# One upright pair fewer in the second pass, new operation times and a new order table in a clustered attention and softplus FFN kernel

## The chip, the cores and the metric

The kernel runs on one core of a Trainium2 chip. The metric is the device time of one execution in microseconds (us). Before the change three runs gave 825.47 us as their median, from 823.66 to 826.16.

## The reference

Attention in which a query sees only the keys of its own cluster, and behind it a feed-forward layer (FFN) with softplus. With 4 batches, 8 heads, 768 positions, head size 64 and 16 clusters, cut to what is computed:

```python
q_n, k_n, c_n = (x / (norm(x) + 1e-6) for x in (q, k, centroids))
q_assign = argmax(einsum('bhsd,hcd->bhsc', q_n, c_n), -1)     # k_assign likewise
mask = q_assign[:, :, :, None] == k_assign[:, :, None, :]
scores = where(mask, q @ k.T / 8, -1e9)
attn = exp(scores - max(scores)); attn = attn / (sum(attn) + 1e-9)
x = (attn @ v).transpose(0, 2, 1, 3).reshape(3072, 512)
h = x @ w_in                                                  # 3072 x 2048
out = (max(h, 0) + log1p(exp(-abs(h)))) @ w_out               # 3072 x 512
```

Products of float32 operands are made from pairs of float16 halves: each operand is cast to a high half, and the rest is subtracted into a low half.

## The kernel before

**The work.** A *pass* is half the queries of one batch: 3 of its 6 blocks of 128 queries. There are 8 passes. Within a pass, each of the 8 heads gives 3 *tiles* (one block of 128 queries against all 768 keys), so there are 192 tiles, numbered `t` in the order pass, head, block. Tiles 0 to 23 are the first pass, 24 to 47 the second. A tile is named by head and block: `s_3_5` is tile 35. Behind the attention of a pass come its FFN1 (`ffn1`, L1205: 16 blocks of 24 matmuls of `h`), softplus (`softplus`, L1234) and FFN2 (`ffn2`, L1280: `o`), which run beside the attention of the next passes.

**Two forms of a tile.** `scores` (L1044) makes the scores of a tile and `attend` (L1125) weights the values with them.

- The *ordinary* form: four matmuls of scores (L1064, `s`), the row maximum on VectorE (L1080, `negm`), the exponential on ACT (L1086), a cast to the high half (`ph`, the cast of L298, on ACT unless moved) and a subtraction for the low half (`p`, L1100, on POOL unless moved). When both tiles of a pair (`t`, `t + 1`) are done, one DMA turns the pair's halves (L1110, `pt<-phl`), and 18 matmuls of float16 halves weight the values (L1148 to L1150).
- The *upright* form (`upright`, L947): two matmuls give the scores of the high halves alone (L957, `m`), VectorE takes their maximum (L969, `negu`), TensorE turns the 128 maxima from a column into a row (L976, into the PSUM tile `turned`), and ACT or VectorE copies that row, scaled, into a spare row of the turned queries (L982 or L984, `qt<-turned`; the operation `u`). Twelve matmuls then give scores that are already shifted and already turned (L996 and L997, `u`), the exponential goes straight to float32 probabilities, and six records of float32 matmuls weight the values (L1144). No cast, subtraction or DMA is needed.

`UPRIGHT` (L33) lists the pairs in upright form: 0 to 17, so tiles 0 to 35. The copy of L976's result must be done before the twelve matmuls. `turned` is one PSUM tile with four places, `turned[:, hk[2] % 4]` (L972).

**The masks.** `nearest` (L561) assigns keys and queries to their clusters with chains of VectorE operations (L593 to L613), for each pair of heads of keys and each four heads of queries; `keep` (L920) and `clusters` (L709) drop clusters without a key. A DMA (`fill`, L553) clears the spare row of queries whose tiles are ordinary but share a group of heads with upright ones.

**The weights** of the FFN come as float64 and are made float16 halves in steps (`prep_weights`, L377) in the first part of the run.

**The order.** All engines execute their instructions in the order in which the program emits them. Each piece of work is a generator that yields operations, waits and ring requests. The class `Order` (L110) runs them: the table `PLAN` (L44) gives, two base-36 digits at a time, the number of the channel whose next operation is emitted (3304 entries). So the table sets the order on every engine, on the SP queue (which issues the DMAs) as well. Operations carry a cost in ns with which `Order.run` keeps a model time per engine; it is used for one thing while emitting: where the model sees a gap on TensorE of over 400 ns, `warm` (L271) puts dummy matmuls (L277, *fillers*) there. A ring (`ring`, L305) makes a channel wait until an earlier user of the same place is done; it holds the emission back, not the chip.

`either` (L288) gives an operation two engines; its key in `SWAPPED` (L39) picks the second. A `cast` (L295) is such an operation: ACT first, POOL second.

Of the kernel before, what the change touches and what calls it, by code (L numbers as in the profile page):

```python
# [29 lines left out]
ROWS = EXTRA + 1  # L30
UP = 8
UPRIGHT = (0, 1, 2, 3, 4, 5, 6, 7, 8, 9, 10, 11, 12, 13, 14, 15, 16, 17)
# [6 lines left out]
SWAPPED = ('g0_3', 'g0_5', 'g1_1', 'g2_5', 'g6_6', 'g6_7', 'g7_1', 'g7_2', 'g7_4', 'g7_7', 'gh1_6', 'gh2_4', 'gh3_1', 'gh6_7', 'gh7_0', 'gh7_2', 'gh7_3', 'gh7_5', 'gh7_6', 'gh7_7', 'k0_0', 'k0_1', 'k14', 'k18', 'k22', 'kT0_0_0', 'kT0_2_1', 'kT1_2_0', 'kT1_2_1', 'm12_2_0', 'm12_3_0', 'm20_4_0', 'm8_2_0', 'm8_3_0', 'p100', 'p101', 'p103', 'p136', 'p38', 'p39', 'p40', 'p42', 'p45', 'p46', 'p47', 'p59', 'p61', 'p64', 'p67', 'p71', 'p72', 'p79', 'p82', 'p85', 'p89', 'p90', 'p92', 'ph58', 'ph62', 'ph83', 'ph86', 'ph87', 'q0_0_0', 'qT1_1', 'u1', 'u11', 'u13', 'u21', 'u23', 'u27', 'u31', 'u33', 'u35', 'v8', 'vh14', 'vh18', 'w15', 'w19', 'w20', 'w23', 'w29', 'wh17', 'wh24', 'wh29', 'wh30', 'wh7', 'wh9', 'x0_2', 'x2_0', 'xh0_3', 'xh1_3', 'xh2_3', 'xh3_0', 'xh3_3', 'zk10', 'zk12', 'zk16', 'zk18', 'zk2', 'zk20', 'zk4', 'zq0_1', 'zq8_2')  # L39
# [5 lines left out]
    "020306c30004050cd10a0000000000000000000101d300d4d20005c4060607070c050100d50001010101d1d1d106d2d2d1d2d6d2d1c5"  # L45
    "0101010101d8d706060c07d1d1d7d2d1d1d1d106d2d1d2d20a0606060606d2d1d2d20101c305d906dadad2d2c4c5d1d10106dcc4d107"
    "d10606c51f1fd2d21h1hd21fd2c608081f05080b0b0bc70adb0908c80b1h1j1j1h1f1f1j1l1l1h1h1jc4c3c3c51g1n1l1j1n1i080808"
    "1n090909c31j1l1p1l081n1p0ac61k070a1l09c30808c7080cc41r1r0b0b0b0b1n1p1pc908cacb0b1t1r1r0cdddd1m0b1t0909091n1p"
    "1pc51t1o1rc81t1rc90bdf090909091vdedhc4c5dfdhdhdh1v1q1q1q1qdidididjdidg1x1t1t1v1v1q1q1scc1qdkcd1x1z1z1x1vca1x"
    "1v1u1z1xc7c6c61zc61xc8c7c7c6c721211w23231z21211z1y210d252023ce0bcfc9cac8cbcc21caca25252723c822c9c9c8ca2723c9"  # L50
    "23252927270d2b2222222925cdce25242b2b29272d29260d0dcccbcccecd2d2729292fcf222b28ccce2f2h2f0d2d2f2d2bcb22cccgch"
    "ci2h2j2a0d0d0dcgcg2b2dcf0dcf0d0dcd2j2c2h2d2f2e0dcf0dcf0d0d22cjcd2fcbcb2h2e2e2e2l2j2j0d0d2l2n2nchci2echcgch2g"
    "2h2h2j2l2n2lcgcgck2jch2nce2p2p2i2l2k2p2l2r2ncicicjci2p2rcdchcl2ncjcj2m2p2t2r0eckckckck2t2p2rcj2e2ecicmcjce2o"
    "2r2r2v2v2t2q2t2v2t2q2q2qcl2x0e0e0e2v2tck2q2q2s2v2v2x2z2z2x2xcmclcmclcm2ucn2q2z312x312w0e0e0e0e0e0e0eco2z2x2z"
    "cl2z330e333131cl2y310fcncn0ecncz33353531cmcmcpcq33czcncococo33dncn35cz37370f0f0fcococrczdododn35303937320e0e"
    "0e0e333537dncz0hdododo3232323439czcp32cqcpcqcpcq32323537390f0f3b3936dqdqdqczcpcp3739crcq3b0fcrcrcrcr393d0fcz"
    "3bcz3b0ecs3d3d3b0f0f0f3dczdrdr0h3bdsds0f0fdrdr0hcqdr383d0i3d3f3f3aczctcscsdscs3f3h3f3f3c3jcz3edt3h3jcscs0gcu"
    "0i0i0i3h3ld03hductct3h3hdu3educz3j0g3n3e3e3educzd0ctcu3l3ndt0i3j3l3pdwdwct3e3edud0cu0g0j0kcucu3l3n3ndwczczdx"
    "3gdx0i3p0i0icz3rczctcucv3l3j3l3p3t3p0g3ndxczdx0i3r3iczdxd03p3pcvdydy3t3r3v0idycz3kdz0jcvcv3tcz3xcvdz3te03md0"
    "0j3vcvcw3t3rdz3x3r3t3v3z3zczdzdze1e1e1e10k0k0k3x3ocze2cw3q3qcz413q3qcwcw0i3ze2e2e2cxcze33qd00n3x0i0i3ve3cwcz"  # L60
    "cwe2d0cze5e53x3s3v3x3qe3e4d0410mcye5czczcxcxcxcxcxe40g3u0ke5e5e6d0e7e741410ke7cz0k0k0k0k0k413z3z410k0n0n3q0n"
    "d0cze9e9e90m0m0ld0e9e9e8d0ea3w0g0g0g0gcycy0gcycy0g0g0gcyd03yd040e80g0g0g0g0ld0420od0424242424242ebeb0n0n0n0n"
    "0n0n0n0n0l0l0n0kd0d04343434343ecd0cz454545454545ecczed4747474747cz494949494949edd0eeczefef4b4b4b0o0oedd04d4d"
    "4defefd00l0l0l0l4f4f0l0ld04b4b4d4d4f444h4h4h4hd0egeg4j4j4j464dcz0l0l0l0l4h4l4l4f4fefczeheheh48cz4a4hcz0l4n4n"
    "cz4l4p0pcz0l4ceieieicz4p4e4e4l4l4j4j4lej4neieiejej4e4e4p4p4pczd0cz4g0p0pek4e4e4eekekek4n4nekczelel4r4r4r4iee"
    "4p4t4t4tczd0elel4v4v4r4r4k4x4x4t4t4v4v4v4x4mczemem4t4z4zczemem51514zczenen4o0p534q4qen4x4x4xcz51d04q4q4q4q53"
# [116 lines left out]
def tile_cluster_attention__then__softplus_ffn(  # L183
# [1050 lines left out]
    def softplus(pi, f, hp, hk):  # L1234
# [31 lines left out]
        if not two:  # L1266
            yield cast(f"gh{pi}_{fp}", 830, 1290, gh[:, 0], g)
# [138 lines left out]
```

## Time and profile before

| what | value |
|---|---|
| median of 3 runs | 825.47 us |
| the profiled execution's own time | 827.26 us |
| its span in the trace | 825.4 us |
| TensorE matmul (PE) busy | 809.5 us, 7919 instructions |
| VectorE (DVE) busy | 522.1 us |
| ScalarE (ACT) busy | 537.0 us |
| GpSimd (POOL) busy | 458.7 us |
| granted TensorE clock | 1.0 in every stretch of 20 us |

How to read the rows that follow: in a group (`L1080 DVE ... x156 | 148.3, 953 | 57.3 <-PE`) stand line, engine, operation, output and inputs with shapes, the count, then the busy us, the mean ns of one, and the idle us just ahead of the group's instructions with what ended most of it. In a timeline a row is start (us), length (us), engine, line. In a table of stages a row is the stretch, its length, then busy us and count of PE, PEld (weight loads), DVE, ACT and POOL, then the granted clock, the share of the DMA engines and GB/s. Matmuls overlap, so their work is taken from start to next start, and not from the length.

### The profile page before, as it was taken

What the parts mean: (1) busy time and instruction counts of PE and PEld (TensorE: products, weight loads), DVE (VectorE), ACT (ScalarE), POOL (GpSimd) and SP (SyncE); (2) the same over time, 40 slices, a digit from 0 to 9 for tenths busy, and PEclk for the clock granted to TensorE, in tenths of its full rate; (3) what the DMA queues carried; (4) which work ended last, traced back from release to release, by engine and by line L of the source; (5) the groups of instructions that cost most, each with busy time, mean ns of one, the idle gap of its engine ahead of it and who ended that gap; (6) DMA issues with size and microseconds to landing.
All of it is one profiled execution on the core that took longest, in us unless ns stands there. A gap on an engine that the chain in (4) does not pass through costs nothing.

```text
span 825.4 us, 19143 instructions
## 1 busy us (share of the span) xinstructions
PE 809.5 (98%) x7919; PEld 525.8 (64%) x7919; DVE 522.1 (63%) x909; ACT 537.0 (65%) x830; POOL 458.7 (56%) x341
## 2 busy tenths in 40 slices
PE   7999999999999999999989999999999999999998
PEld 7888987655666666566656656556666656655554
DVE  6789998877876877666785557577555444332222
ACT  5776789865877777558578677767766668622220
POOL 4753556444756576655667685677576666611120
PEclk9999999999999999999999999999999999999999
DMA  8986768999999999998799999999889787530001
GB/s 236 239 197 138 204 158 218 213 212 197 179 177 174 179 207 201 212 197 170 153 166 172 183 171 208 199 197 172 171 158 163 136 138 134 118 54 14 26 1 39
DMA packets 389816, 133.69 MB, mean 162 GB/s; under 512 B 367072, under 2 KB 382688, under 8 KB 389728
## 3 DMA queue, kind: packets, MB, share of 16 engines
q1 hardware_dynamic: 389728, 132.46, 81.3%
q8 instruction: 62, 1.02, 0.5%
q14 instruction: 26, 0.21, 0.1%
HBM read 35.68 MB, written 6.29 MB: 51 GB/s over the span
## 4 chain that ended last, share of the span: by engine, by line
PE 86%; DVE 5%; DMA 4%; ACT 2%; issue 1%; POOL 0%; SPq 0%; DVEq 0%; ACTq 0%; POOLq 0%
PE s L1064 11%; PE h L1219 9%; PE h L1221 9%; PE h L1220 9%; PE o L1303 9%; PE o L1305 9%; PE o L1304 9%; PE mbank L1144 5%; PE mbank L1150 3%; PE mbank L1148 3%; PE mbank L1149 3%; DMA pt<-phl 2%; DMA kt<-kn 1%; PE u L996 1%; PE u L997 1%; PE m L957 1%
## 5 line engine op out<-in xcount | busy, mean ns | idle before, releaser
L1100 POOL TENSOR_TENSOR phl<-p,phl 128x768 f16<-128x768 f32 x133 | 220.3, 1664 | 145.5 <-ACT phl L298 98.8
L1080 DVE TENSOR_REDUCE negm<-s 128x1 f32<-128x768 f32 x156 | 148.3, 953 | 57.3 <-PE s L1064 57.0
L1086 ACT ACTIVATE p<-s,negm 128x768 f32<-128x768 f32 x156 | 139.5, 895 | 68.7 <-DVE negm L1080 56.4
L1221 PE MATMUL h<-xT,wi 128*128 128x384 f16 x512 | 166.8, 326 | 0.0
L1220 PE MATMUL h<-xT,wi 128*128 128x384 f16 x512 | 166.7, 326 | 0.0
L1219 PE MATMUL h<-xT,wi 128*128 128x384 f16 x512 | 166.7, 325 | 0.1
L1303 PE MATMUL o<-wo,gh 128*128 128x512 f16 x376 | 142.4, 379 | 0.4 <-DVE ot L1352 0.4
L1305 PE MATMUL o<-wo,gh 128*128 128x512 f16 x376 | 142.5, 379 | 0.0
L1304 PE MATMUL o<-wo,gh 128*128 128x512 f16 x376 | 142.4, 379 | 0.0
L298 ACT CAST phl<-p 128x768 f16<-128x768 f32 x151 | 123.8, 829 | 19.2 <-DMA pt<-phl 16.3
L1252 DVE SCALAR_TENSOR_TENSOR fg<-fa,h 128x384 f32<-128x384 f32 x128 | 70.1, 549 | 103.9 <-ACT fa L1241 95.9
L1240 ACT ACTIVATE fa<-h 128x384 f32<-128x384 f32 x128 | 62.3, 487 | 111.0 <-PE h L1221 110.6
L1064 PE MATMUL s<-kt,qt 128*128 128x384 f16 x624 | 127.0, 326 | 2.4 <-ACT p L1086 2.4
L1272 POOL TENSOR_TENSOR gh<-fg,gh 128x768 f16<-128x768 f32 x54 | 89.3, 1657 | 29.5 <-ACT gh L298 28.2
L1148 PE MATMUL mbank<-vb,pt 128*128 128x65 f16 x936 | 101.3, 192 | 0.5 <-DMA pt<-phl 0.5
L1149 PE MATMUL mbank<-vb,pt 128*128 128x64 f16 x936 | 101.4, 192 | 0.0
L1150 PE MATMUL mbank<-vb,pt 128*128 128x65 f16 x936 | 101.0, 194 | 0.0
L1148 PEld LDWEIGHTS <-pt 128*128 128x128 f16 x936 | 86.9, 98 | 14.2 <-DMA pt<-phl 2.6
L1149 PEld LDWEIGHTS <-pt 128*128 128x128 f16 x936 | 86.3, 97 | 11.4
L1150 PEld LDWEIGHTS <-pt 128*128 128x128 f16 x936 | 86.5, 97 | 0.0
L1064 PEld LDWEIGHTS <-qt 128*128 128x128 f16 x624 | 58.3, 98 | 43.2 <-issue 3.1
L1221 PEld LDWEIGHTS <-wi 128*128 128x128 f16 x512 | 49.9, 98 | 33.2
(180 smaller groups left out, 1307.3 us busy)
## 6 DMA issues: line engine op xcount, KB each, us to landing
wo<-in_moe_w_in_dram SPq DMA_DIRECT2D x16, 512.0 KB, 5.4
wo<-in_moe_w_out_dram SPq DMA_DIRECT2D x14, 512.0 KB, 4.3
out_dram<-ot SPq DMA_DIRECT2D x23, 256.0 KB, 2.6
rawk<-in_k_dram SPq DMA_DIRECT2D x15, 384.0 KB, 4.2
rawq<-in_q_dram SPq DMA_DIRECT2D x15, 384.0 KB, 4.4
rawv<-in_v_dram SPq DMA_DIRECT2D x12, 384.0 KB, 4.0
rawv<-in_v_dram SPq DMA_DIRECT2D x8, 192.0 KB, 6.1
pt<-phl SPq DMA_TRANSPOSE x78, 5.9
```

Source lines behind the costliest of these rows:

```text
L1064: nc.tensor.matmul(st[:, j, :SH], qt[:, s, i], kt[:, s, NT // 2 * j : NT // 2 * (j + 1)], start=(s == 0), stop=(s == 1),)
L1080: yield op("DVE", 950, lambda: nc.vector.tensor_reduce(negm, st[:, :, :SH], AX.XY, ALU.max, negate=True))
L1100: lambda e: e.tensor_tensor(phl[:, u, 1], p32, phl[:, u, 0], ALU.subtract),
L1148: nc.tensor.matmul(av, pt[:, 0, c], vb[:, c, D : 2 * D + 1], start=(c == 0), stop=False)
L1149: nc.tensor.matmul(av[:, :D], pt[:, 0, c], vb[:, c, :D], start=False, stop=False)
L1150: nc.tensor.matmul(av, pt[:, 1, c], vb[:, c, D : 2 * D + 1], start=False, stop=(c == NT - 1))
L1219: nc.tensor.matmul(hp, w[0], x[0], start=(c == 0), stop=False)
L1220: nc.tensor.matmul(hp, w[0], x[1], start=False, stop=False)
L1221: nc.tensor.matmul(hp, w[1], x[0], start=False, stop=(c == NP - 1))
L1303: nc.tensor.matmul(po, g[0], wo[:, f, 0, 0], start=(f == f0), stop=False)
L1304: nc.tensor.matmul(po, g[0], wo[:, f, 0, 1], start=False, stop=False)
L1305: nc.tensor.matmul(po, g[1], wo[:, f, 0, 0], start=False, stop=(f == f0 + NF // 2 - 1))
```

## The change

Pair 17 (tiles 34 and 35: head 3, blocks 4 and 5, in the second pass) is made in ordinary form. The costs of some operations are set to other numbers. The ring of turned maxima has size 1, so that a turning is emitted only after the copy of the one before is. `SWAPPED` (103 keys, now 143) and `PLAN` (3304 entries, as before) are replaced as a whole.

```diff
-UPRIGHT = (0, 1, 2, ..., 14, 15, 16, 17)
+UPRIGHT = (0, 1, 2, ..., 14, 15, 16)
...
-SWAPPED = ('g0_3', 'g0_5', 'g1_1', 'g2_5', 'g6_6', 'g6_7', ...
+SWAPPED = ('g0_1', 'g0_5', 'g0_7', 'g1_1', 'g1_7', 'g2_0', ...
...
-    "020306c30004050cd10a0000000000000000000101d300d4d20005c4060607070c050100d50001010101d1d1d106d2d2d1d2d6d2d1c5"
+    "020306c30405000a07d10101d3d4000000000000000000000006060101d5000100d1d1d2d201060101010cd2d1d1d1060101d101d1d1"
...
-        yield cast(f"wh{step}", 655, 890, part[:, 0], val)
+        yield cast(f"wh{step}", 655, 720, part[:, 0], val)
...
-            ("DVE", 640),
+            ("DVE", 690),
...
-        yield cast(f"vh{n}", 830, 1290, vb[:, :, :, D : 2 * D], vf)
+        yield cast(f"vh{n}", 830, 870, vb[:, :, :, D : 2 * D], vf)
...
-            ("DVE", 950),
+            ("DVE", 1000),
...
-        yield either(f"zk{n}", last[:2], ("ACT", 310), mark, **here)
+        yield either(f"zk{n}", last[:2], ("ACT", 370), mark, **here)
...
-        hk = yield from ring("mT", 4)
+        hk = yield from ring("mT", 1)
         ps = turned[:, hk[2] % 4]
...
-        yield either(f"u{t}", ("ACT", 250), ("DVE", 190), shift)
+        yield either(f"u{t}", ("ACT", 265), ("DVE", 290), shift)
...
-            yield cast(f"ph{t}", 830, 1290, parts[0], p32)
+            yield cast(f"ph{t}", 830, 870, parts[0], p32)
...
-        yield cast(f"xh{pi}_{pr}", 510, 690, by_head[0], x32)
+        yield cast(f"xh{pi}_{pr}", 510, 510, by_head[0], x32)
```

The other casts and subtractions get the same new numbers (1290 to 870, 950 to 1000, 540 to 560; 220 to 270 for the marks of the first queries). The last two numbers of a cast are its costs on ACT and on POOL.

What the new tables come to, counted in the two programs: L1064 has 632 matmuls where it had 624, L957 68 (72), L976 34 (36), L996 and L997 204 each (216), L1144 204 (216), L1148 to L1150 948 each (936), and the fillers of L277 are 175 (200). 34 more casts stand on POOL, and 32 fewer on ACT: 18 of `phl`, 4 of `gh`, 5 of `xn`, 2 of `wo`, 2 of `wi`, 2 of `kn` and 1 of `vb`. VectorE has 9 more subtractions of L1272 (19 where 10 stood) and 3 fewer of L1100 (20 where 23 stood). The SP queue has one more transposition of a pair and one more clearing of a spare row. All 34 turnings of maxima (L976) stand in the order of their tiles. The rows below show two places, as the programs emit them.

On VectorE, what stood before where tile 35 (head 3, block 5) has its maximum; `negu` is an upright tile's maximum, `mx_k8`, `eq_k8` and `best_k8` are key masks, `wo` is a weight step:

```order
L969 TENSOR_REDUCE negu_3_4_1996<-m_3_4_1944 128x1
L597 TENSOR_REDUCE mx_k8_1993<-sim_k8_1928 128x12
L414 TENSOR_SCALAR wo_120<-wo_120 128x512
L418 SCALAR_TENSOR_TENSOR wo_120<-wo_120 128x512
L603 TENSOR_TENSOR eq_k8_2036<-sim_k8_1928,mx_k8_1993 128x192
L969 TENSOR_REDUCE negu_3_5_2044<-m_3_5_2034 128x1
```

After, on the same engine at the same tile (`negm` is an ordinary tile's maximum, `p32` the probabilities in float32, `phl` the pair of their halves, `fg` of the softplus):

```order
L1080 TENSOR_REDUCE negm_3_5_2008<-s_3_5_2000 128x1
L1252 SCALAR_TENSOR_TENSOR fg_0_1_1970<-fa_0_3_1985,h_0_3_1972 128x384
L609 TENSOR_TENSOR eq_k8_2010<-eq_k8_2010,tab_78 128x192
L1100 TENSOR_TENSOR phl_3_4_2001<-p32_3_4_1998,phl_3_4_2001 128x768
L1100 TENSOR_TENSOR phl_3_4_2001<-p32_3_5_2037,phl_3_4_2001 128x768
L611 TENSOR_REDUCE best_k8_2067<-eq_k8_2010 128x12
```

The maximum of tile 35 became one of full scores, and the two low halves of tiles 34 and 35 (L1100) came in on VectorE behind it, ahead of the last operations of a key mask.

On TensorE, before, where tiles 15 and 16 (head 5, blocks 0 and 1) are turned:

```order
L1144 MATMUL mbank_117<-rawv_4_132,ptf_4_0_1165 128x65 x6
L976 MATMUL turned_116<-eye32_100,negu_5_1_1188 65x128
L976 MATMUL turned_116<-eye32_100,negu_5_0_1172 65x128
L996 LDWEIGHTS kt_4_593
L996 MATMUL u_4_2_1219<-qt_4_0_610,kt_4_593 128x128
```

After, at the turning of tile 16 on the same engine (`m` are the scores of an upright tile's maximum):

```order
L1144 MATMUL mbank_117<-rawv_4_132,ptf_4_0_1127 128x65 x6
L976 MATMUL turned_116<-eye32_100,negu_5_1_1160 65x128
L957 LDWEIGHTS qt_4_0_549
L957 MATMUL m_6_0_1199<-kt_6_543,qt_4_0_549 128x384
L957 LDWEIGHTS qt_4_0_549
```

Tile 15's turning, which stood right behind that of 16, now stands 31 rows ahead of it, and other work lies between the two.

More of the change, by code (lines that the diff above doesn't have):

```diff
@@ L50 @@
[L50 to L54, printed above, removed]
@@ new lines @@
+    "1r1v0909df09dh1vdic90c0c0cc51r1tcac71q1q1q1qdhdhdh1v1t1x1xdidic6di1vc81t1qc91q1s1v1z1x1zc71x1vc908dgcbdjdec7"
+    "c71u211z1x1z1x21c8c6c81wcc0b1z2121ca23231zc8cdc7ca1y25210dc6c6cecb25202321c9cacacac8cc2327222325272922222222"
+    "2229c9cd23252b2b270d0d2725dk1qcf0d2924cececc2dcd2dc9cecbcc25272927262b2b2fcfcbcf2f2929280d2d0d2bcccbcb0d0d0d"
+    "0d2a2h0d2hcfcdce2d2f2b2d2c2jcgcgcgch0d0dcfcecf2j0d2d2e2e2e2e2f2h2f2h2f0d0d0d2j2j2l2l2n2ncicjch2ecdci0d2g2l2l"
+    "2h2h2n2jcgcg2p2n2jchcicgck2pcjchcicjcccj2i2p2l2l2k2p2n2r2rchchclcici2ncd2e2m2t2p2r0e222tckckck2pcm2rcjckcj2o"
@@ L644, in prep_k @@
         else:
-            yield cast(f"kh{n}", 830, 1290, n1[:, :, :D], kf)
+            yield cast(f"kh{n}", 830, 870, n1[:, :, :D], kf)
             yield either(
@@ L648, in prep_k @@
                 ("POOL", 1640),
-                ("DVE", 950),
+                ("DVE", 1000),
                 lambda e: e.tensor_tensor(n1[:, :, D:], kf, n1[:, :, :D], ALU.subtract),
@@ L697, in low_half @@
             ("POOL", 910),
-            ("DVE", 540),
+            ("DVE", 560),
             lambda e: e.tensor_tensor(dst[:, :, D:], src, dst[:, :, :D], ALU.subtract),
@@ L767, in prep_q @@
         if pi == 0:
-            yield cast(f"qh{sfx}", 850, 1290, n1[:, :, D:], qf)
+            yield cast(f"qh{sfx}", 850, 870, n1[:, :, D:], qf)
             yield either(
@@ L771, in prep_q @@
                 ("POOL", 1640),
-                ("DVE", 950),
+                ("DVE", 1000),
                 lambda e: e.tensor_tensor(n1[:, :, :D], qf, n1[:, :, D:], ALU.subtract),
@@ L802, in prep_q @@
         )
-        yield either(f"zq{sfx}", last[:2], ("ACT", 310), mark_queries(n2[:, :, ROWS : ROWS + NCL], sim), **here)
+        yield either(f"zq{sfx}", last[:2], ("ACT", 370), mark_queries(n2[:, :, ROWS : ROWS + NCL], sim), **here)
         wide = ROWS if n < H else D
@@ L863, in first_q @@
             ("POOL", 910),
-            ("DVE", 540),
+            ("DVE", 560),
             lambda e: e.tensor_tensor(lo, x, hi, ALU.subtract),
@@ L878, in first_q @@
         )
-        yield either(f"zq0_0_{u}", last[:2], ("ACT", 220), mark_queries(n2[:, part, ROWS : ROWS + NCL], sim), **here)
+        yield either(f"zq0_0_{u}", last[:2], ("ACT", 270), mark_queries(n2[:, part, ROWS : ROWS + NCL], sim), **here)
         yield wait("al", 2 * u)
@@ L1031, in upright @@
                 ("POOL", 1640),
-                ("DVE", 950),
+                ("DVE", 1000),
                 lambda e: e.tensor_tensor(parts[1], p32, parts[0], ALU.subtract),
@@ L1094, in scores @@
         phl, phlk = pair[t // 2]
-        yield cast(f"ph{t}", 830, 1290, phl[:, u, 0], p32)
+        yield cast(f"ph{t}", 830, 870, phl[:, u, 0], p32)
         yield either(
@@ L1098, in scores @@
             ("POOL", 1640),
-            ("DVE", 950),
+            ("DVE", 1000),
             lambda e: e.tensor_tensor(phl[:, u, 1], p32, phl[:, u, 0], ALU.subtract),
@@ L1183, in attend @@
             ("POOL", 910),
-            ("DVE", 540),
+            ("DVE", 560),
             lambda e: e.tensor_tensor(by_head[1], x32, by_head[0], ALU.subtract),
@@ L1266, in softplus @@
         if not two:
-            yield cast(f"gh{pi}_{fp}", 830, 1290, gh[:, 0], g)
+            yield cast(f"gh{pi}_{fp}", 830, 870, gh[:, 0], g)
         yield either(
@@ L1270, in softplus @@
             ("POOL", 1640),
-            ("DVE", 950),
+            ("DVE", 1000),
             lambda e: e.tensor_tensor(gh[:, 1], g, gh[:, 0], ALU.subtract),
```

114 lines of the change are left out of this document (57 added, 57 removed).

## Prediction

> **What bounds the kernel now.** I read the page first (busy times and the chain that ended last), then a table of stages of 20 us with each engine's busy time, then the waits of the weight and matmul rows at the turning (L976), then timelines of single tiles.
>
> ```profile
> PE 809.5 (98%) x7919; PEld 525.8 (64%) x7919; DVE 522.1 (63%) x909; ACT 537.0 (65%) x830; POOL 458.7 (56%) x341
> PE 86%; DVE 5%; DMA 4%; ACT 2%; issue 1%; POOL 0%; SPq 0%; DVEq 0%; ACTq 0%; POOLq 0%
> ```
>
> TensorE is busy for 98% of the span and carries 86% of the chain; no other engine passes 65%. So the time is TensorE's own work plus the moments at which it stands. The stages, with busy us of PE, PEld, DVE, ACT and POOL in this order:
>
> ```profile
> 0.00:20.00 20.00, 16.00 (x279) 15.56 (x279) 12.69 (x62) 12.04 (x20) 7.86 (x23) 1.00 0.86 238
> 20.00:40.00 20.00, 18.14 (x259) 16.07 (x260) 15.58 (x30) 13.69 (x24) 15.62 (x12) 1.00 1.00 231
> 40.00:60.00 20.00, 20.00 (x225) 18.91 (x222) 16.53 (x34) 14.16 (x24) 9.14 (x11) 1.00 0.89 216
> 60.00:80.00 20.00, 18.09 (x206) 16.32 (x203) 19.21 (x36) 13.74 (x27) 8.05 (x9) 1.00 0.53 144
> 80.00:100.00 20.00, 19.48 (x220) 18.39 (x217) 17.96 (x28) 14.64 (x25) 10.61 (x9) 1.00 0.79 170
> 100.00:120.00 20.00, 20.00 (x214) 16.91 (x213) 18.48 (x36) 16.10 (x28) 9.85 (x8) 1.00 0.76 198
> 420.00:440.00 20.00, 17.95 (x192) 11.33 (x191) 14.01 (x18) 14.61 (x23) 15.45 (x11) 1.00 0.84 161
> 820.00:825.00 5.00, 2.23 (x21) 1.76 (x18) 0.50 (x2) 0.00 (x0) 0.00 (x0) 1.00 0.15 52
> sum 825.00, PE 809.49 PEld 525.76 DVE 522.08 ACT 537.00 POOL 458.73; mean PE 19.27 PEld 12.52 DVE 12.43 ACT 12.79 POOL 10.92
> ```
>
> TensorE stands 825.00 - 809.49 = 15.5 us: 4.0 in the first stage, 4.3 from 20 to 100 us (the upright tiles), 2.8 at the very end, and 4.4 scattered between, of which 2.05 lie in one stage. The reader should note VectorE from 60 to 120 us: 55.65 of 60 us. There it is nearly as full as TensorE.
>
> **The change part by part.** *Tiles 34 and 35.* One tile's work on TensorE in each form, from starts to next starts, since matmuls overlap:
>
> ```profile
> 88.08 0.49 PE L957 MATMUL m<-kt,qt 128*128 128x384 f16 x2
> 88.40 0.27 PE L976 MATMUL turned<-eye,negu 128*65 128x128 f32 x1
> 88.51 1.45 PE L1144 MATMUL mbank<-rawv,ptf 128*128 128x65 f32 x12
> 89.80 0.22 PE L996 MATMUL u<-qt,kt 128*128 128x128 f16 x1
> 90.47 0.33 PE L957 MATMUL m<-kt,qt 128*128 128x384 f16 x1
> 419.31 0.81 PE L1064 MATMUL s<-kt,qt 128*128 128x384 f16 x4
> 419.96 0.33 PE L1219 MATMUL h<-xT,wi 128*128 128x384 f16 x1
> 420.94 0.19 PE L1148 MATMUL mbank<-vb,pt 128*128 128x65 f16 x1
> 421.48 0.32 PE L1219 MATMUL h<-xT,wi 128*128 128x384 f16 x1
> ```
>
> An upright tile takes one of each of four groups: 0.32 (maxima) + 0.11 (turning) + 1.29 (weighting the values) + 0.67 (scores), or 90.47 - 88.08 = 2.39 us. An ordinary one takes 419.96 - 419.31 = 0.65 for the scores and 421.48 - 420.94 = 0.54 for the values: 1.19 us. Two tiles save 2 x 1.20 = **2.4 us** of TensorE. The bound from the other side is 0, if VectorE sets the pace there.
>
> What the two tiles need in exchange lies on engines with room over the whole span, but not beside the place where they stand. Their path, by the groups of instructions and the table of DMA issues:
>
> ```profile
> L1080 DVE TENSOR_REDUCE negm<-s 128x1 f32<-128x768 f32 x156 | 148.3, 953 | 57.3 <-PE s L1064 57.0
> L1086 ACT ACTIVATE p<-s,negm 128x768 f32<-128x768 f32 x156 | 139.5, 895 | 68.7 <-DVE negm L1080 56.4
> L298 ACT CAST phl<-p 128x768 f16<-128x768 f32 x151 | 123.8, 829 | 19.2 <-DMA pt<-phl 16.3
> L1100 DVE TENSOR_TENSOR phl<-p,phl 128x768 f16<-128x768 f32 x23 | 27.2, 1196 | 1.7 <-POOL phl L1100 0.8 <-ACT phl L298 0.6 <-issue 0.2
> pt<-phl SPq DMA_TRANSPOSE x78, 5.9
> ```
>
> By the rows of the new order (shown with the change), both subtractions now stand on VectorE, and key masks and later maxima are queued behind them. From the last score of tile 35 to its turned halves the path takes at least 0.95 + 0.90 + 0.83 + 1.20 + 5.9 = 9.8 us, if nothing else is in its way. In the new order TensorE has between that score and the first value matmul of tile 34: 24 matmuls of `h` and 12 of `s` (0.1625 each, 0.65 / 4), three upright value groups (1.29 to 1.34 each) and one set of scores (0.67): 5.85 + 4.0 + 0.67 = 10.5 us. Cover of 0.7 us is thin; a queue of 1 to 3 us ahead of any step would stop TensorE, since its instructions go in order. I charge **+1.0**, bounds 0 and +2.5.
>
> *The turning.* Each maximum is turned by TensorE (L976) into one tile, `turned`, and copied away by ACT or VectorE (L982, L984). Although `turned` has four places, the trace shows turnings that wait for the copy of the tile before:
>
> ```profile
> 36.14 0.28 PE L976 MATMUL turned<-eye,negu 128*65 128x128 f32 x1
> 37.04 0.27 ACT L982 ACTIVATE qt<-turned 1x128 f16<-1x128 f32 x1
> 37.36 0.32 PE L976 MATMUL turned<-eye,negu 128*65 128x128 f32 x1 [0.62 <-ACT qt L982]
>   ACT qt L982: 3.2, 6
>   DVE qt L984: 0.9, 2
>   ACT wo L412: 0.6, 1
>   DVE rs L1165: 0.5, 1
> ```
>
> The last four rows (who ended the idle time before L976, us and times) sum to 5.2 us; they count the weight row's idle time too, and the matmul row's own idle time from 20 to 100 us is 4.3. In the order rows shown with the change, tile 16 was turned ahead of 15, side by side. After, tile 15's turning stands 31 rows earlier, and all turnings are in order, apart by at least a group of other work. The wait itself is not taken away: nothing gets a new buffer, each turning now stands behind the copy of the one before, and what is queued behind it is all of TensorE. It is only given cover. In five places (tiles 2, 3, 15, 20, 22) the cover is 0.33 to 0.67 us, where the copy above ended 37.31 - 36.14 = 1.17 us after its turning began, so some 0.6 us each can remain. I take **-2.0** of the matmul row's 4.3; bounds -4.3 and +2 (five places of 0.6 with cover lost elsewhere).
>
> *The fillers.* TensorE runs dummy matmuls (L277) where the order table expects a gap:
>
> ```profile
> 15.56 1.63 PE L277 MATMUL mbank<-ones,eye 128*128 128x120 f16 x28
> 9.71 1.15 ACT L860 CAST qn<-rawq 128x384 f16<-128x384 f32 x2 [2.36 <-DMA rawq<-in_q_dram]
> ```
>
> 28 take 1.63 us, less one's drain of about 0.2: 0.052 each. After has 175 where before had 200: 25 x 0.052 = 1.3 us. Most stand in the first 20 us, where the query load ends the wait at 9.71 us in both (the first transfers are in the same order), so part only turns into idle time: **-0.6**, bounds -1.3 and +0.4 (six more fillers stand ahead of the first key turning).
>
> *Durations, swaps, table.* The new costs move 34 casts from ACT to POOL. Those of probabilities, 18 of the 34, take 0.97 us there (the row below) and 0.83 on ACT; both are off the path, where cover holds. What remains is luck of the new order at the scattered stalls, 4.4 us. The largest:
>
> ```profile
> 420.72 1.79 DVE L613 TENSOR_TENSOR eq_q<-eq_q,best_q 128x192 f16<-128x192 f16 x1
> 424.14 1.69 DVE L929 TENSOR_TENSOR eq_q<-eq_q,al 128x192 f16<-128x192 f16 x1
> 420.65 3.36 POOL L1100 TENSOR_TENSOR phl<-p,phl 128x768 f16<-128x768 f32 x2 [0.47 <-ACT phl L298]
> L298 POOL CAST phl<-p 128x768 f16<-128x768 f32 x5 | 4.8, 968 | 4.3 <-DMA pt<-phl 4.3
> L613 DVE TENSOR_TENSOR eq_q<-eq_q,best_q x14: 348/357/1791, 73.4 to 660.1; 128x192 f16<-128x192 f16 x14
> PE s L1064 <- ACT p L1086: 2.4, 3, 2.1
> ```
>
> Two masks of VectorE ran beside POOL's subtractions and took 1.79 and 1.69 us, where L613 takes 0.357 at the median of 14 (the row with least, median and most): some 2.8 us lost, a maximum late, the exponential late, TensorE stopped for 2.1. The Trainium skill, "SBUF — State Buffer", section "Who interferes with whom", says that VectorE and GpSimd share a pair of ports by an exclusive lock held for a whole instruction, and that VectorE operations with two SBUF inputs contend while those with one do not. The rows agree; by that rule every cast moved to POOL is one more hold of the lock, which speaks against this edit. By its letter each of the 34 could block VectorE for a whole cast, and the sum would be about 829, as in the second rival. By the rows POOL goes from 459 to some 480 us, 5% more, and only one of the 26 mask chains stopped TensorE by 2 us; so I let the better fit and the extra holds nearly cancel: **-1.0**, bounds -4.4 and +4.4.
>
> **The sum.** -2.4 + 1.0 - 2.0 - 0.6 - 1.0 = -5.0 us. The profiled execution took 827.26 us (span 825.4 and 1.9 around it), which would become 822.3. The runs shown have a median of 825.47, 1.8 below it; the same saving gives **820.5**.
>
> **The rivals.** First, VectorE takes the pace from 20 to 120 us. It stands idle there for 12.2 us (100 less the five stages' 87.8), and the new order puts about 3 us more on it by tile 34: two more weight subtractions, two whole key ones, query masks. Against it: it waits rarely for long. If so, the two tiles and the turning give nothing: -0.6 + 1.0 - 1.0, 824.9. Chance 0.20.
>
> Second, slower: the lock. If four more mask chains stop TensorE as at 425 us, 4 x 2.1 = 8.4 in place of the -1.0: -2.4 + 1.0 - 2.0 - 0.6 + 8.4 = +4.4, 829.9. It decides from the third such stall on (-4.0 + 6.3 = +2.3). For it: POOL's added casts; against it: one in 26 now. Chance 0.12.
>
> Third, the order does better: the turning gives 4.3, fillers 1.3, scattered stalls 3, no late halves: -2.4 - 4.3 - 1.3 - 3.0 = -11.0, 814.5. Chance 0.14.
>
> Fourth, the turning is ordered on paper alone, as no buffer changes, and its waits come back: -2.4 + 1.0 - 0.6 - 1.0 = -3.0, 822.5. Chance 0.14. My forecast has 0.40.
>
> **How the numbers follow.** A measurement of this kernel can tell some 0.3%, or 2.5 us: faster is below 823.0, slower above 827.9. Faster: 0.39 of the forecast, 0.14 of the third, 0.09 of the fourth, 0.03 of the first: 0.65. Slower: 0.11 of the second and 0.02 of others: 0.13. Within: 0.22. The range 815 to 827 leaves out half of the third (0.07) and the second (0.12).
>
> **What would show it.** Right: TensorE's busy time falls by 3 to 4 us; L976's releasers sum to under 3.5 us; a wait of TensorE for `pt` near 115 us under 2.5; stage sums from 180 us on unchanged within 2. Wrong: TensorE idle time above 16 us; VectorE above 19 of 20 us in several stages before 120; or waits of 2 us of L1064 or L1148 behind masks stretched over 1.5 us.

## The result, and the profile after

The changed kernel takes 831.75 us (median of 4 runs, 830.59 to 832.53) where the kernel before takes 825.82 in the same comparison: a ratio of 1.0082, 95% interval 1.0066 to 1.0099. It is slower by some 6 us. Forecast were 820.5 us and a range of 815 to 827.

In four stages (0 to 120, 120 to 200, 200 to 440, 440 to 817 us), with busy us of PE, PEld, DVE, ACT and POOL as in the table of the prediction, first the kernel before:

```profile
0.00:120.00 120.00, 111.70 (x1390) 102.16 (x1391) 100.45 (x222) 84.37 (x145) 61.13 (x70) 1.00 0.80 200
120.00:200.00 80.00, 79.47 (x722) 50.45 (x720) 63.72 (x114) 57.65 (x91) 38.91 (x31) 1.00 0.98 208
200.00:440.00 240.00, 236.23 (x2428) 146.22 (x2426) 177.93 (x274) 173.18 (x260) 154.94 (x106) 1.00 0.98 181
440.00:817.00 377.00, 376.85 (x3341) 222.49 (x3339) 178.44 (x298) 221.81 (x336) 203.74 (x136) 1.00 0.70 130
```

The same of the changed kernel, behind the first line of its page:

```profile
PE 810.2 (98%) x7884; PEld 523.8 (63%) x7884; DVE 534.9 (64%) x912; ACT 520.5 (63%) x802; POOL 479.8 (58%) x368
...
0.00:120.00 120.00, 112.80 (x1360) 101.44 (x1361) 103.96 (x223) 83.92 (x144) 63.13 (x76) 0.99 0.80 202
120.00:200.00 80.00, 73.42 (x676) 44.94 (x677) 69.22 (x105) 51.36 (x83) 45.43 (x34) 0.98 0.89 190
200.00:440.00 240.00, 236.22 (x2406) 146.99 (x2405) 176.36 (x275) 162.26 (x241) 166.67 (x121) 1.00 0.99 184
440.00:817.00 377.00, 377.00 (x3375) 223.45 (x3373) 183.18 (x307) 222.92 (x338) 204.60 (x139) 1.00 0.70 133
```

Up to 120 us the changed kernel is the better one: TensorE stands 7.2 us where it stood 8.3, and the first matmul of `h` starts at 101.7 us where it started at 103.7. From 120 to 200 us it stands 6.6 us where it stood 0.5, and the granted clock drops: it is 0.93 from 160 to 180 us and 0.98 from 180 to 200, which comes to some 3.5 us at half. (It is 0.91 from 20 to 40 us as well.) VectorE's busy time grows there from 63.7 to 69.2 us, POOL's from 38.9 to 45.4. No wait for a turned pair near 115 us is to be found. The longest waits of TensorE from 100 to 200 us, after (before, the same question has one answer, a key transposition of 0.5 us):

```profile
PE sim_k L579 <- DMA kt<-kn: 1.5, 1, 1.5
PE h L1219 <- DVE gh L1256: 1.4, 1, 1.4
PE h L1219 <- DVE fg L1252: 1.3, 2, 0.8
PE mbank L277 <- DVE x L1173: 1.3, 1, 1.3
PE cnt L720 <- DVE fg L1252: 0.8, 1, 0.8
```

Most of it is VectorE. Two places show why, in timelines of the changed kernel (start, length), with the SP queue's rows between 162 and 170 us and the matmuls behind the last stall:

```profile
129.07 3.87 POOL L1100 TENSOR_TENSOR phl<-p,phl 128x768 f16<-128x768 f32 x2
129.49 1.96 DVE L418 SCALAR_TENSOR_TENSOR wo<-wo 128x512 int32<-128x512 int32 x1
131.37 1.68 DVE L669 TENSOR_SCALAR kn<-eq_k 128x192 f16<-128x192 f16 x1
134.40 0.32 PE L1219 MATMUL h<-xT,wi 128*128 128x384 f16 x1 [0.78 <-DVE fg L1252]
...
158.86 3.46 DVE L1100 TENSOR_TENSOR phl<-p,phl 128x768 f16<-128x768 f32 x2 [0.30 <-issue]
159.27 2.24 POOL L1272 TENSOR_TENSOR gh<-fg,gh 128x768 f16<-128x768 f32 x1
161.47 2.35 POOL L650 TENSOR_TENSOR kn<-rawk,kn 128x768 f16<-128x768 f32 x1
163.30 0.32 PE L1219 MATMUL h<-xT,wi 128*128 128x384 f16 x1 [1.38 <-DVE gh L1256]
...
162.39 3.64 SPq L317 DMA_TRANSPOSE pt<-phl  x1
169.46 0.33 SPq L312 DMA_DIRECT2D wraw<-in_moe_w_out_dram  x1
169.89 4.92 SPq L317 DMA_TRANSPOSE kt<-kn  x2
...
176.36 0.42 PE L579 MATMUL sim_k<-cents,kt 128*128 128x32 f16 x10 [1.55 <-DMA kt<-kn]
177.17 0.58 PE L1304 MATMUL o<-wo,gh 128*128 128x512 f16 x1
177.55 0.63 PE L1305 MATMUL o<-wo,gh 128*128 128x512 f16 x1
```

At 129 us POOL subtracts two tiles. Beside it VectorE's weight step (L418) and key mark (L669), 0.69 and 0.24 us at the median of the kernel before, take 1.96 and 1.68, the softplus behind them is late, and TensorE stands. At 159 us two subtractions of VectorE run beside two of POOL; all four are stretched. The DMA that turns the pair starts late, a weight load that needs its place starts late, and two key transpositions behind it on the SP queue are late too: the stall of 1.55 us that ends at 176.36. Behind it the matmuls of `o` start every 0.43 us, not every 0.22, for 3.2 us.

The longest stop of all comes later, at 353 us:

```profile
PE o L1303 <- DVE ot L1352: 2.5, 2, 1.9
```

There VectorE's mark and mask of a group of queries (L849 and L929, at 350.6 and 352.2 us) stand beside POOL's subtractions, take 1.56 and 1.64 us, and hold up the sum (`ot`, L1352) that frees a place for `o`. The same 2.5 us stand in the traces of five more runs of this order; with clears in the place of POOL's subtractions they are gone, with copies 0.6 us are left.

I call *stretch* the time that VectorE's instructions take above the tenth percentile of their line and operand layout, where it is some 0.1 us or more. It is 37.5 us in the trace of before and 43.1 after; between 100 and 200 us it is 2.8 and 15.9. (The sizes hang on the counting: by line and shape, with every small difference, they are 46.4 and 53.7, and 5.0 and 19.1. The contrasts stay.)

### The profile page after: what moved, and what is told of

The parts are those of the page before. It is cut to its first block, busy times and chain, and to the rows that moved or that the text cites. A ratio compares the mean times of both kernels' runs of the same rounds, so it can differ in the third digit from the quotient of the medians.

```text
span 830.7 us, 19061 instructions
## 1 busy us (share of the span) xinstructions
PE 810.2 (98%) x7884; PEld 523.8 (63%) x7884; DVE 534.9 (64%) x912; ACT 520.5 (63%) x802; POOL 479.8 (58%) x368
## 4 chain that ended last, share of the span: by engine, by line
PE 67%; POOL 4%; DMA 3%; DVE 3%; issue 2%; ACT 1%; SPq 0%; POOLq 0%; ACTq 0%; DVEq 0%
PE s L1064 9%; PE o L1303 8%; PE o L1305 8%; PE o L1304 8%; PE h L1219 8%; PE h L1221 8%; PE h L1220 8%; PE mbank L1150 3%; PE mbank L1148 3%; PE mbank L1149 3%; POOL phl L1100 2%; DMA pt<-phl 2%; POOL phl L298 1%; DMA wraw<-in_moe_w_out_dram 1%; DMA rawk<-in_k_dram 1%
## 5 line engine op out<-in xcount | busy, mean ns | idle before, releaser
L1100 POOL TENSOR_TENSOR phl<-p,phl 128x768 f16<-128x768 f32 x138 | 230.0, 1675 | 112.3 <-ACT phl L298 81.7
L1080 DVE TENSOR_REDUCE negm<-s 128x1 f32<-128x768 f32 x158 | 150.1, 953 | 70.9 <-PE s L1064 69.8
L1086 ACT ACTIVATE p<-s,negm 128x768 f32<-128x768 f32 x158 | 141.5, 896 | 65.9 <-DVE negm L1080 62.0
L1252 DVE SCALAR_TENSOR_TENSOR fg<-fa,h 128x384 f32<-128x384 f32 x128 | 69.9, 549 | 99.1 <-ACT fa L1241 96.8
L1064 PE MATMUL s<-kt,qt 128*128 128x384 f16 x632 | 128.4, 326 | 0.7 <-ACT p L1086 0.7
L298 ACT CAST phl<-p 128x768 f16<-128x768 f32 x135 | 110.3, 828 | 16.5 <-DMA pt<-phl 14.5
L1148 PE MATMUL mbank<-vb,pt 128*128 128x65 f16 x948 | 102.5, 192 | 0.9 <-DMA pt<-phl 0.7
L1150 PE MATMUL mbank<-vb,pt 128*128 128x65 f16 x948 | 102.2, 194 | 0.0
L1272 POOL TENSOR_TENSOR gh<-fg,gh 128x768 f16<-128x768 f32 x45 | 77.2, 1715 | 40.2 <-ACT gh L298 39.8
L1148 PEld LDWEIGHTS <-pt 128*128 128x128 f16 x948 | 88.0, 98 | 13.8 <-DMA pt<-phl 2.1
L1149 PEld LDWEIGHTS <-pt 128*128 128x128 f16 x948 | 87.4, 97 | 11.3
L1150 PEld LDWEIGHTS <-pt 128*128 128x128 f16 x948 | 87.5, 97 | 0.0
L1064 PEld LDWEIGHTS <-qt 128*128 128x128 f16 x632 | 58.6, 98 | 39.6 <-issue 1.5
```

Of the source, the lines that this page charges most:

```text
L1064: nc.tensor.matmul(st[:, j, :SH], qt[:, s, i], kt[:, s, NT // 2 * j : NT // 2 * (j + 1)], start=(s == 0), stop=(s == 1),)
L1080: yield op("DVE", 950, lambda: nc.vector.tensor_reduce(negm, st[:, :, :SH], AX.XY, ALU.max, negate=True))
L1100: lambda e: e.tensor_tensor(phl[:, u, 1], p32, phl[:, u, 0], ALU.subtract),
L1148: nc.tensor.matmul(av, pt[:, 0, c], vb[:, c, D : 2 * D + 1], start=(c == 0), stop=False)
L1149: nc.tensor.matmul(av[:, :D], pt[:, 0, c], vb[:, c, :D], start=False, stop=False)
L1150: nc.tensor.matmul(av, pt[:, 1, c], vb[:, c, D : 2 * D + 1], start=False, stop=(c == NT - 1))
```

## The experiments

Ratios are to the kernel before, run on the same chip in between. Times of different rows differ by the chip as well; compare the ratios.

| run | ratio (95% interval) | median us |
|---|---|---|
| changed kernel | 1.0082 (1.0066 to 1.0099) | 831.75 |
| after_writes_only | 0.9947 (0.9934 to 0.9960) | 819.62 |
| before_writes_only | 0.9969 (0.9959 to 0.9979) | 821.92 |
| after_writes_690_980 | 1.0032 (1.0010 to 1.0054) | 828.03 |
| after_two_copies | 0.9998 (0.9986 to 1.0009) | 824.71 |
| after_casts_back | 1.0183 (1.0169 to 1.0196) | 839.37 |
| no_late_fillers | 1.0091 (1.0077 to 1.0106) | 833.11 |
| casts_back_no_late_fillers | 1.0118 (1.0100 to 1.0136) | 835.37 |
| before_engines_of_after | 1.0488 (1.0458 to 1.0517) | 865.76 |
| after_pair17_upright | 1.0141 (1.0119 to 1.0164) | 836.72 |
| before_pair17_ordinary | 1.0104 (1.0082 to 1.0125) | 834.03 |
| before_40_fillers | 1.0059 (1.0036 to 1.0082) | 829.30 |
| after_then_before | 1.0049 (1.0033 to 1.0066) | 827.88 |
| then_before_no_late_fillers | 1.0077 (1.0062 to 1.0092) | 832.38 |
| keys_first_no_late_fillers | 1.0096 (1.0081 to 1.0110) | 834.08 |
| after_weight_later | 1.0105 (1.0085 to 1.0125) | 834.17 |
| before_maxima_first | 0.9998 (0.9986 to 1.0010) | 824.73 |
| maxima_first_ten_fillers_less | 0.9993 (0.9984 to 1.0002) | 824.26 |

**What the collisions cost.** POOL's subtractions (all but those of `x` and of the first half keys) go through one helper, which writes instead of reading; the low halves are left out:

```diff
+    def rest(e, dst, x, hi):
+        if e is not nc.gpsimd:
+            e.tensor_tensor(dst, x, hi, ALU.subtract)
+            return
+        one = (slice(None),) + (slice(0, 1),) * (len(dst.shape) - 1)
+        e.tensor_tensor(dst[one], x[one], hi[one], ALU.subtract)
+        e.memset(dst, 0.0)
+        e.memset(dst, 0.0)
```

> The changed kernel; each subtraction that stands on POOL (except those of x and of the first half keys) is replaced by one of a single column and two clears of the same tile, which write and don't read, so POOL is busy about as long (two clears of 768 at some 0.74 us) and waits for the same inputs; the low halves of those operands are left out (zero). Theory A: VectorE's stretch falls from 43 to under 12 us, TensorE's lost time between 120 and 200 us from 10.9 to under 4, the time to 822 to 826. Theory E (VectorE is simply full there, with or without POOL): the stretch goes, but the time stays within 2 us of 831.75.

> The kernel before with the same replacement of POOL's subtractions (low halves of those operands left out). Theory A: its stretch (37.5 us in sum) lies mostly behind 200 us, where VectorE has room, and cost TensorE little but the stall at 425 us: 822 to 825, and the difference between the two kernels of this pair turns to the changed one being 0 to 4 us faster. Theory E: within 1 us of before, and the difference between the pair stays at 4 us or more in favour of the kernel before.

> The changed kernel; only the 22 subtractions that stand on POOL between entries 690 and 980 of the order table (some 120 to 200 us) are replaced by one of a single column and two clears, as in the run where all of them were; the low halves of these 22 are left out. Replacing all gave 12 us. Theory A with its place (VectorE has no room between 120 and 200 us, and the collisions there cost most): 822 to 826. Theory A without it (collisions cost alike everywhere; 22 of some 190 are replaced): 829 to 831.

POOL stays as busy (486.8 us for 479.8 in the changed kernel, 465.2 for 458.7 in the kernel before), and VectorE's stretch falls to 9.6 us in the changed kernel and to 5.3 in the kernel before. The changed kernel gains 1.35%, or 11 us, the kernel before 0.31%, or 2.6. So theory A holds in kind, with more gained in the changed kernel than it forecast, and E falls. The zeros in the low halves are no rival: the value matmuls take 192 ns with and without them. Without collisions the order of the two turns round: the changed kernel is 0.22% (1.8 us) the faster one, with intervals that just touch. That is near the 2.4 us of the two tiles, but the pair differs in all the other parts of the change too. Replacing only the 22 subtractions between some 120 and 200 us, out of 237, gives 0.5% (4 us, with a wide interval): more than their share, less than theory A with its place asked. The first two stages of after_writes_only:

```profile
0.00:120.00 120.00, 115.26 (x1399) 103.49 (x1399) 104.01 (x229) 87.74 (x150) 68.24 (x137) 1.00 0.83 209
120.00:200.00 80.00, 76.60 (x693) 46.02 (x693) 56.43 (x105) 53.77 (x87) 48.64 (x87) 1.00 1.04 202
```

From 120 to 200 us VectorE needs 56.4 us, not 69.2. TensorE still stands 3.4 us there, and 0.9 in the kernel before without collisions: 2.5 us of that stage's loss of 6.1 are not the collisions. The rest of the 11 us lies elsewhere: TensorE stands 2.5 us less up to 120 us, 3.1 less from 200 to 440, and the clock is 1.00 throughout.

**Whether one operand read is enough.** In the helper, POOL copies `x` to `dst` twice.

> The changed kernel; each subtraction on POOL (except those of x and of the first half keys) is replaced by two copies of its first operand to the same place, so POOL reads one operand and not two, for about as long (some 0.87 us each); the low halves are replaced by copies. Theory H (any instruction of POOL that reads SBUF stretches VectorE's, as the Trainium skill has it, in SBUF — State Buffer, section Who interferes with whom): VectorE's stretch stays above 30 us, the time 829 to 833. Theory I (only POOL's reading of two operands does; casts, which read one, stretched 1 of 4): stretch under 15 us, 819 to 824.

The stretch falls to 30.3 us only, as theory H has it, but the time to 824.7, just above what theory I has; neither holds as a whole. One line of VectorE tells why (least, median and most ns): first before, then the changed kernel, the run with clears, the run with copies.

```profile
L609 DVE TENSOR_TENSOR eq_k<-eq_k,tab x12: 249/350/1636, 122.1 to 558.7; 128x192 f16<-128x192 f16 x12
```

```profile
L609 DVE TENSOR_TENSOR eq_k<-eq_k,tab x12: 251/1001/1726, 121.5 to 565.1; 128x192 f16<-128x192 f16 x12
```

```profile
L619 DVE TENSOR_TENSOR eq_k<-eq_k,tab x12: 251/259/934, 117.4 to 552.1; 128x192 f16<-128x192 f16 x12
```

```profile
L617 DVE TENSOR_TENSOR eq_k<-eq_k,tab x12: 251/259/911, 119.9 to 559.2; 128x192 f16<-128x192 f16 x12
```

At worst the operation waits about as long as POOL's instruction lasts: 1.73 - 0.25 = 1.48 us beside subtractions of 1.65, 0.91 - 0.25 = 0.66 beside copies of some 0.87. (The 0.93 in the run with clears stood beside a subtraction of `x` of 0.92, which the helper leaves as it is.) The Trainium skill, "SBUF — State Buffer", section "Who interferes with whom", says that a VectorE operation with two SBUF inputs contends with a GpSimd instruction that reads SBUF and that the shared ports are an exclusive lock held for the whole instruction; both runs agree with it. The copies differ from the subtractions in two things, one operand for two and half the length; that the longest waits in both traces end with the instruction in progress speaks for the length. A subtraction on POOL cut into two halves, which follows from this, was not tried.

**The casts.** The keys of the casts in `SWAPPED` are those of before:

```diff
-SWAPPED = (..., 'gh0_4', ..., 'ph46', 'ph50', 'ph52', ...)
+SWAPPED = (...)
```

> The changed kernel with its order table, but every cast is on the engine on which the kernel before has it (42 casts from POOL back to ACT, 8 the other way). Theory C (the casts on POOL make its subtractions late and hold the shared ports): 826 to 828. Theory A (subtractions, not casts, stretch VectorE's operations; only 4 of VectorE's operations ran beside a cast alone, 1 of them was stretched): within 1.5 us of 831.75, and the stretch of VectorE's operations stays above 35 us in sum. Theory D (ACT has no room either): 833 or more.

That run had 420 fillers, where the changed kernel has 175, since the table's own clock then saw gaps, so it does not tell. Without fillers behind 110 us (`if gap > WARM_FROM and od.free["PE"] < 110e3:`):

> The changed kernel without the fillers behind 110 us of the order table's own time (11, at 195.9 us; 164 stay). In its trace these fillers wait 1.3 us for VectorE's x (L1173), since they write the PSUM bank that x is read from, and take 0.6 us after that. Theory F (late fillers cost, not help: what stands behind them was ready): 829.5 to 830.5. Theory A: what stands behind them would have waited nearly as long: 831.0 to 831.8.

> As the run with the casts back on their engines of before, but without the fillers behind 110 us; that run had 420 fillers where the changed kernel has 175, by the order table's own time, and 245 of 0.052 us are 12.7 us, so it did not tell the casts apart. Theory C (the casts on POOL cost): 826 to 829. Theory A (they neither cost nor gain): 830 to 833. Theory D (ACT has no room for them where they stood, so moving them was a gain): 835 or more.

Theory F falls: without the 11 late fillers the changed kernel is not faster (1.0091 against 1.0082, intervals overlap). Against that run the casts on ACT cost 0.27% (2.2 us; the intervals just overlap), in the range of theory D. But ahead of 110 us that run still has 272 fillers where its partner has 164, 108 of 0.052 us or 5.6 us of TensorE, and 6.8 us at half clock behind 113.8 us; so it doesn't price the casts either. What speaks against theory C are the traces: 4 of VectorE's operations ran beside a cast alone, and 1 of them was stretched; and after_writes_only, which keeps every cast on POOL, has lost most of the stretch. In later runs, where it is not said otherwise, the number and place of fillers is fixed by a table.

> The kernel before, its order table and its fillers as they are, but every cast, subtraction, mark and copy on the engine on which the changed kernel has it (90 keys of the table of swaps differ beside those of pair 17). Theory A1 (the engines chosen bring POOL and VectorE together: 9 more subtractions of softplus halves on VectorE, 34 more casts on POOL): 829 or more. Theory A2 (it is the order; the engines alone do nothing): within 2 us of before, 823.5 to 827.5.

This is 40 us, and neither A1 nor A2 is told by it. Before 100 us, where TensorE of the kernel before stands 8.3 us at a clock of 1.00, it now stands 13.5 us at a mean clock of 0.90; the rest is lost behind. An operation that changes its engine lands in the other queue at a place that nobody chose, and what stands behind it waits. Engines and order can only be judged together.

**Pair 17 alone, both ways.** `UPRIGHT` with or without 17, in the other kernel's order, the operations of tiles 34 and 35 exchanged in place.

> The changed kernel with its order, engines and fillers, but pair 17 (tiles 34 and 35) upright again, with the added operations of the two tiles put into the order beside their neighbours. By the sum TensorE's work grows by 2.4 us. Theory B (the late halves of these two tiles set off the loss): 829 or less. Theory A (they are not its cause): 833 to 835.5.

> The kernel before, its order, engines and fillers, with pair 17 alone in ordinary form: the operations of tiles 34 and 35 that fall away leave the order, the new ones stand beside their neighbours (both subtractions on POOL), and the two value steps stand five and four of TensorE's steps later, so that they have some 11 us of cover. By the sum -2.4 us: 822 to 824 (theory K). Theory J: the shift brings new collisions, 826 or more. Theory B (late halves): a wait for pt of over 1 us near 115 us.

In the changed order pair 17 in upright form is slower by 0.59% (4.9 us by the medians; the profiled spans differ by 3.0): the two tiles gain what the sum gives, and more, and theory B falls for the changed order. In the order of before the same edit costs 8.6 us, as theory J has it. Its trace:

```profile
137.46 0.83 ACT L296 CAST kn<-rawk 128x768 f16<-128x768 f32 x1 [3.05 <-DMA rawk<-in_k_dram]
...
139.15 1.12 PE L1062 MATMUL s<-kt,qt 128*128 128x384 f16 x3 [4.55 <-ACT p L1084]
...
133.70 0.90 SPq L310 DMA_DIRECT2D rawk<-in_k_dram  x1
```

The added pair transposition stands on the SP queue ahead of a key load, and waits 3.8 us for POOL's subtraction. The load starts at 133.7 us where it started at 126.6, ACT's cast of those keys waits 3.05 us for it, an exponential stands behind the cast, and TensorE stands 4.55 us for that. Behind it the granted clock is 0.95 (120 to 140 us) and 0.88 (140 to 160), some 6.8 us at half. The wait of over 1 us for `pt` that theory B asks for is not there: the longest is 0.7.

**A shift.** `FILLERS` gets 40 more ahead of the first block of `h`.

> The kernel before with 40 more fillers (2.1 us of TensorE) ahead of its first block of h, at some 103 us; order, engines and its other fillers are unchanged. Theory J (the order owes its time to an exact alignment; any shift brings new collisions): over 829.5, or under 825. Theory K (it takes a shift as it is): 2.1 us more than before, 826.5 to 828.5.

4.9 us more (interval 3.0 to 6.8), where 2.1 were put in: by its middle in J's range, by its interval in K's too. This shift costs about double itself; so the kernel before has some fit to its own timing, but doesn't stand on a needle's point.

**Repairs of the order.** First the changed order up to entry 700 of the table and that of before behind it; then, in the changed kernel, two transpositions ahead of the weight load, and that weight step later:

> The changed kernel, but with its order table only for the first 700 of 3304 entries (up to the value matmuls of tiles 34 and 35, some 115 us); from there on the operations stand in the order, and on the engines, of the kernel before. Theory A (POOL's subtractions run beside VectorE's mask and weight steps between 120 and 200 us and stretch them, where VectorE has no room): that stretch is due to the order behind entry 700, so the loss of 8.5 us between the 4th and the 16th block of h goes, the 2 us by which the changed kernel leads at 120 us stay: 823.5, between 822.5 and 825. Theory B (the thin cover of tiles 34 and 35, and what their late halves set off): both tiles stand within the first 700 entries, so it stays at 829 to 832. Theory C (the casts moved to POOL): most stand behind entry 700 and go back, so 824 to 826, not told apart from A by this run.

> As the run with the order of before from entry 700 on, without the fillers behind 110 us; that run had 50 fillers at 135 us which first waited 1.8 us for x. Theory A (the loss lies in the order behind entry 700, and that run's remaining 3.2 us over the kernel before is the fillers at the seam): 823 to 825. Theory B (tiles 34 and 35 set off a delay that stays): 826.5 or more.

> The changed kernel without late fillers, and with one change of order on the SP queue: the two transpositions of keys (head pairs 10 and 12) stand ahead of the weight load of step 30 (wraw), which waits until the transposition of a pair of tiles has landed and has a place free; in the kernel before one of the two stood ahead of it. Theory G (the key transpositions are late because they queue behind that waiting load; this gave the stall of 1.7 us at 174.5 us and the half clock behind it, 1.9 us): 2 to 3.6 us below the run without late fillers. Theory A alone (the subtraction of those keys on POOL, stretched, made them late): under 1 us below it.

> The changed kernel, its engines and fillers; weight step 30 is moved: its load behind the two transpositions of keys on the SP queue, its two operations on ACT behind the next exponential, halves and softplus, those on VectorE likewise. Theory G2 (ACT and VectorE stood 3.4 us behind this step's load at 170 us, and TensorE's stall of 1.7 us and the half clock of 1.9 us behind it came from there): 827 to 829.5. Theory A alone: the collisions make another wait of it, within 1.5 us of the changed kernel.

The mixed order recovers 0.33% of the 0.82% (2.7 us), no more; without late fillers (164, where the mixed order had 232) it loses that again, with two spells of half clock of 3.4 us each in its trace. Theory A's place fails in both: it had 822.5 to 825 and 823 to 825. B's second range fits (826.5 or more), though pair 17 alone speaks against B's cause. So the order of before is not good behind entry 700 by itself: it seems fitted to what stood ahead of it. With the keys first, TensorE's wait at 175 us is not gone but has another name:

```profile
175.05 0.66 ACT L412 ACTIVATE wo<-wraw 128x512 f32<-128x512 f32 x1 [4.82 <-DMA wraw<-in_moe_w_out_dram]
...
178.41 0.38 PE L1303 MATMUL o<-wo,gh 128*128 128x512 f16 x1 [3.22 <-DVE ot L1347]
```

ACT's weight operation now waits 4.82 us for its load, VectorE behind it, and TensorE for VectorE. Theory G falls as a repair. Moved behind other work, the same step makes the kernel no faster either (1.0105): G2 falls. In the first of these edits another wait ended last, and in the trace of the second TensorE stands 2.96 us at 189 us instead.

**A version that beats both?** In the kernel before, four mask operations behind two maxima at 421 us; and ten fillers less at 59 us. Then the kernel before, profiled a second time.

> The kernel before, its engines and fillers; at 421 us four operations of a query mask (L613, L849, L929, L930), which ran beside POOL's subtractions and stood ahead of two maxima, stand behind these two on VectorE. Before, TensorE stood 2.2 us at 425.7 for the exponential behind those maxima. Theory L (a stall taken out where little follows is kept): 1.2 to 2.2 us under before, 822.5 to 824. Theory J (the shift brings other waits): within 0.8 us of before, or above.

> As the run with the maxima first, and without the ten fillers at 59.4 us (0.52 us): these write the PSUM bank from which VectorE reads its row sums (L1165), which waited 1.64 us for them, the next maximum stood behind that, and TensorE's scores waited 1.5 us for the maximum. Theory L: 1 to 1.7 us under the other run. Theory J: the shift by that much at 60 us costs more than it gives, above the other run.

> The kernel before, unchanged, profiled a second time. If the stall of 2.2 us at 425 us belongs to the kernel, it stands here again, and the run with the maxima first must have lost as much elsewhere. If it belongs to the one execution (827.26 us, 1.8 above the median), it is absent and the span is near 823.5.

Neither differs from before by more than the uncertainty, so theory L falls. The stall at 425 us is gone from the trace of the first, but the time is the same, and the second profile (824.35 us, span 822.6) says why: from 420 to 440 us TensorE waits there for nothing but

```profile
PE mbank L1148 <- DMA pt<-phl: 0.2, 1, 0.2
```

The stall of 2.1 us on which part of the prediction rests stands in one of the two profiled executions of that kernel. No version here that computes everything beats the kernel before.

## Why the prediction was wrong

- *Tiles 34 and 35, -2.4*: right in the changed order, where pair 17 alone gives -3.0 (spans) to -4.9 (medians). In the order of before the same two tiles cost 8.6 us, so their price is not theirs alone.
- *Their late halves, +1.0*: no wait for `pt` came. TensorE stood 0.55 us at 117 us for the softplus on VectorE instead (`h` behind L1252), and 0.4 us in two places for a key mask (L603).
- *The turning, -2.0*: about right in sum, with a misreading. The 4.3 us that it was taken from are all of TensorE's standing from 20 to 100 us; the matmul row of L976 itself has 1.9. That standing is 2.5 us after, 3.9 in the second profile of before. The releasers of L976, weight row included, sum to 1.8 + 1.2 + 0.4 = 3.4 us after, 5.2 before:

```profile
  ACT qt L982: 1.8, 4
  DVE negu L969: 1.2, 3
  DVE qt L984: 0.4, 1
```

- *The fillers, -0.6*: of the size of the noise. By 20 us the second profile of before has lost as much as the changed kernel.
- *Durations, swaps, table, -1.0 with bounds of 4.4 either way*: this is the step that failed: "so I let the better fit and the extra holds nearly cancel". It was the term with the largest unknown, and I gave it the middle. Worked back, the result needs 831.75 - 825.82 = 5.9, plus the 4.0 that the other four terms give if they hold: about +10, beyond its bound. The runs put 11 - 2.6 = 8.4 us of it down to collisions between POOL's reads and VectorE, each difference uncertain by some 2 us.
- The second rival was the mechanism and got 0.12, though the holders were POOL's subtractions, not the added casts that it named. It asked for four masks stopping TensorE by 2.1 us each. One stop is of its kind, that of 1.9 us at 353 us; beside it weight steps, marks and VectorE's own subtractions were stretched too, and from 100 to 200 us the stops were of 0.8 to 1.5 us, through the softplus that frees `h` and through late loads. Its condition, "only one of the 26 mask chains stopped TensorE", was read from a stall that the second profile does not have. Nor does the number of inputs divide VectorE's operations as the prediction has it: the marks L669 and L849 have one input, and took 1.68 and 1.56 us beside subtractions.
- The first rival had the right symptom at the wrong place: from 60 to 120 us VectorE was as full as before (55.6 of 60 us), but from 120 to 200, where the FFN has begun while masks and weight steps go on, it went from 63.7 to 69.2. The table of stages shown in the prediction skips from 120 to 420 us.

Of the signs named in advance, TensorE idle above 16 us came true (20.5), against the forecast; so did, for it, L976 under 3.5 us, no wait for `pt` near 115 us, and stages from 180 us on within 2 of before. TensorE's busy time should have fallen by 3 to 4 us and rose by 0.7, part of it matmuls at half clock.

What stays open: why the new order brings POOL and VectorE together more often just there. The new durations, the swaps and the search that made the table were not told apart, since no run here changes one and keeps a fitting order; the casts on POOL have no price of their own. Some 2.5 us between 120 and 200 us are lost without collisions as well; two attempts at the wait at 175 us only moved it.

## What to carry to other kernels

Where in-order queues of five engines are fitted to each other by a table, the new table can be the largest term of the sum, as here, and is no remainder: price it by the stage in which a second engine has no room, with the whole stretch of that engine's instructions there. VectorE's two-input operations and POOL's reads of SBUF should be planned as one shared resource, and one profiled execution can hold a stall that the next one does not: profile twice before a term rests on it.

## What the runs showed of the hardware

A VectorE operation that was stretched ends shortly after the POOL instruction that was in progress when it started. In the changed kernel L849, 0.23 us alone, starts at 611.66 us, 0.04 behind a subtraction of 1.64, and takes 1.71. Counted over three traces, for VectorE's operations with both inputs in SBUF and the one-input `TENSOR_SCALAR` and copies there, with 0.1 us above the tenth percentile of line and layout as a stretch: 51 of 95 that ran beside POOL's subtractions were stretched (0.54 us for each us of overlap), 66 of 118 beside copies (0.33), 6 of 80 beside clears (0.09), and none that ran beside nothing (111 to 139 in each trace).

TensorE's granted clock fell to half in spells of 3.4 us, or of 6.8, as behind the stall of 4.55 us. In the changed kernel they begin at 20.2 us, in a stall of 1.78, and at 177.2, behind that of 1.55; behind the stall of 1.92 at 353 us, and that of 2.05 at 426 us in the kernel before, there is none. They stand in some executions only: of the changed kernel's four, two had a mean clock of 1.000 (830.59 and 831.63 us) and two of 0.996 (831.86 and 832.53).
